# Sliding-window attention and a PReLU feed-forward on one core: the seven-product scheme begins one block earlier, and the sums it needs are made in borrowed rooms

## The chip, the cores and the metric
One core of a Trainium2 chip runs one program. The metric is device time in microseconds; the runs shown before the change gave 881.37, 882.29 and 882.43, median 882.29. The profiled execution took 882.02 us, of which 880.3 us lie between its first and last instruction (the span).

## The reference
```python
scores = scale * q @ k^T, masked to 0 <= i - j < 64      # 8 batches x 8 heads, 576 tokens, head 64
x = softmax(scores) @ v, heads side by side               # 4608 tokens x 512
h = x @ w_in                                              # 512 -> 2048
g = max(h, 0) + alpha * min(h, 0)
out = g @ w_out                                           # 2048 -> 512
```
Everything is fp32. The weights come as 64-bit numbers and are turned into fp32 in the kernel.

## The kernel before, in words
**Tiles and blocks.** The 4608 tokens are 36 tiles of 128; four tiles are a block, so there are 9 blocks, numbered 0 to 8 here ("the third block" is block 2). A block's hidden layer has 16 slices f of 128.

**Split numbers.** Each fp32 operand is held as a high part and a low part (`xh`/`xl`, `win_h`/`win_l`, `gh`/`gl`, ...), and a product is three matmuls: high-high, high-low, low-high.

**A cell** (`cell`, line 883) is one slice f of one block done plainly: 12 matmuls of 512 columns into one PSUM bank (line 896, called H here), then slopes on ACT (line 798), the PReLU on DVE (805), the high part on ACT (811), the low part on POOL (815), and 12 matmuls of 512 columns into the four output banks (line 832, called o).

**A pair** (`pair`, line 971) does two slices q = f/2 at once by a Strassen-like scheme: seven half products of 6 matmuls with 256 columns (line 1010, called P: 42 of them) in the place of eight. It uses two banks (`bx`, `by`), a few adds on DVE (1037), copies on ACT (1045, 1047), the sums of tokens that `attend` makes for a paired block (lines 726 to 776) and five entries of sums of `w_in`, 256 KB each, which are streamed from DRAM for each pair (line 988) into five rooms ("ring"). Four of these rooms are pieces of `win_h`/`win_l`, free once the sums 6 and 7 are made and the last plain block has used its slices 12 to 15; the fifth is a room of the eighth sum.

**The sums of `w_in`** (`combine(q)`, line 921, q = 0 to 7) each take four rooms of 128x512: two totals (930), four short DVE operations (935 to 938), two high parts on ACT (942), two low parts on POOL or DVE (945), and six stores to DRAM from SP's queue (950, 954).

**Blocks.** Block 0 and 1 get their attention in block 0 (t = 0 to 7) by PE transposes; weights are converted meanwhile. `W0 = 3`: blocks 0 to 2 are plain, blocks 3 to 8 paired.

**Visits.** From block 2 on the attention of a block is done inside earlier blocks, at two places of each (`stays`, lines 1130 to 1136, and 1160 to 1172). A visit is, in PE's order, the scores of one tile (64 small matmuls, line 578, called s), the values of two earlier tiles (64 matmuls, line 699, called AV), and the scores of another tile. `put_behind` fixes this order; a hidden slice two further on is put behind the visit's end.

**Who sets the order.** `Plan` is a list scheduler with a written cost of each step: it takes steps in order of time, hands out banks (four, `bank`: 4 to 7) and rooms, and the instructions are emitted in the order of its times. `take` and `give` are a step's rooms; `behind` fixes an order of starts, not of ends; `want` is a due time. The early steps have due times and first times written out (`DUE`, `BEGIN`, `HELD`). A tile's values hold their bank until its token operands are written (lines 710 to 776).

**The end.** Each block's four output tiles are copied (868, 870) and stored (873). The rooms ("os") are four at first; two are passed on to other uses by the eighth sum, so two are left for the last blocks.

Of the kernel before, what the change touches and what calls it, by code (L numbers as in the profile page):

```python
# [9 lines left out]
F32 = mybir.dt.float32  # L10
# [260 lines left out]

STAYS = (10, 2)
FAT = 10
W0 = 3
SHORT = 93.0
TSETS = (0, 3)
LAGS = (16.0, 19.0)
EARLY = (14.0, 18.0, 23.0, 28.0)
FIRST, PACE, TURN, LONG = 20.0, 5.6, 112.0, 97.0

# [2 lines left out]
def banded_attention_then_prelu_ffn(  # L283
# [65 lines left out]
    def weight(name, f):  # L349
        f0 = max(x for x in parts_of[name] if x <= f)  # L350
        return parts_of[name][f0][:, f - f0, :]

    xh = const.tile([P, NP, RING * P], F32R, name="xh")
    xl = const.tile([P, NP, RING * P], F32R, name="xl")

    stock = dict(bank=[4, 5, 6, 7], o=[0, 1, 2], q=["q0", "q1"], k=["k0", "k1"], v=["v0"], w=[0, 1],
                 mix=["pt0"], clean=[], pt=[], new=[], kk=[], T0=[], T1=[], ring=[], u2=[], u=[0, 1], reg0=[0], reg1=[1], ring6=[("h", 6)],
                 ring7=[("l", 6)], ring8=[("h", 7)], ring9=[("l", 7)], g=["g0", "g1"], gh=["gh0", "gh1", "gh2"], gl=["gl0", "gl1"],
                 raw=["u0", "u1", "u2"], val=["e0", "e1"], low=["e2", "e3"], os=[])
    pts = dict(pt0=const.tile([P, NH, P], F32, name="pt_0"))  # L360
# [4 lines left out]
    plan = Plan(stock)  # L365
    plan.stock["o"].append((WARM + 1.0, 3))
    spare = ps.tile([P, P], F32, tag="b3", name="spare")
    nought = xl[:, 0, (RING - 1) * P:].bitcast(F32)
    nc.vector.memset(nought, 0.0)
    plan.idle = lambda _: nc.tensor.matmul(spare, nought, nought, start=True, stop=True)  # L370
    step = plan.step
# [4 lines left out]
    def room(b, shape, dtype, name):  # L376
        return sb.tile(shape, dtype, tag=str(b.at), name=name)
# [103 lines left out]
    def attend(t, by_pe, want, loads_behind=(), behind=(), soon=math.inf):  # L481
# [218 lines left out]
                                         d["pt"][:, u * NP + e, h * W:(h + 1) * W], start=True, stop=True)  # L700

        def x_high(_):
            nc.scalar.copy(xh[:, :, xs], d["av"])

        def x_low(_):
            nc.vector.tensor_tensor(out=xl[:, :, xs], in0=d["av"], in1=xh[:, :, xs].bitcast(F32), op=ALU.subtract)  # L706
            if not paired:
                d.clear()

# [77 lines left out]
    def parts(t):  # L787

        return [slice(0, E // 2), slice(E // 2, E)] if t == NT - 1 else [slice(0, E)]

    def behind(ts, f, d, done, hb, want_o, cols, coarse=True):
# [68 lines left out]
        if f == NF - 1:  # L860
            for i, t in enumerate(ts):
                for x in parts(t):
                    sbuf, os = Buffer("os" if len(parts(t)) == 1 else "g", 1), {}

                    def copy(e, t=t, x=x, sbuf=sbuf, os=os):
                        os[0] = room(sbuf, [P, x.stop - x.start], F32, f"os_{t}_{x.start}")
                        if e == ACT:
                            nc.scalar.copy(os[0], po[t][:, x])
                        else:
                            nc.vector.tensor_copy(os[0], po[t][:, x])  # L870

                    def store(e, t=t, x=x, os=os):
                        (nc.scalar if e == ACT else nc.sync).dma_start(out[t * P:(t + 1) * P, x], os[0])

                    m = len(parts(t))
                    c = step({DVE: (0.33, 0.42)} if x.start else {ACT: (0.28, 0.39)} if m == 2 else
                             {ACT: (0.48, 0.59), DVE: (0.6, 0.69)}, copy, [whole[t]], take=[sbuf],
                             give=[ob[t]], want=want_o + 3 + i)
                    step({ACT: (0.4, 0.4)} if x.start else {SP: (0.4, 0.4)}, store, [c], give=[sbuf], moved=0.8 / m)
                    if t < NBLK:  # L880
                        begun.append(c)

    def cell(ts, f, want_h, want_o):
        plan.group = "c", f, ts[0]
        n = len(ts)
        nt = n * P
        d = {}
        xs = slice((ts[0] % RING) * P, (ts[0] % RING) * P + nt)
        hb = Buffer("bank", 1)

        def hidden(_):
            d["h"] = ph = bank(hb, [P, NBLK * P], F32, f"h_{ts[0]}_{f}")
            k = 0
            for wt, xt in (("win_h", xh), ("win_h", xl), ("win_l", xh)):
                for c in range(NP):
                    nc.tensor.matmul(ph[:, :nt], weight(wt, f)[:, c * P:(c + 1) * P], xt[:, c, xs],  # L896
                                     start=(k == 0), stop=(k == 3 * NP - 1))
                    k += 1

        xb = [st[t]["x"] for t in ts]  # L900
        s0 = step({PE: ({2: 1.46, 4: 2.72}[n], {2: 1.55, 4: 2.87}[n])}, hidden,
                  [st_done[t] for t in ts] + cv[2 * f]["done"], take=[hb], want=want_h)
        first[ts[0] // NBLK, f] = s0
        for b in xb:
            b.uses = NF
        s0.give += xb
        if ts[0] // NBLK == W0 - 1:
            s0.give += regions[f // 2]
        behind(ts, f, d, [s0], hb, want_o, range(n))
# [11 lines left out]
    def combine(q):  # L921
        plan.group = "s", q, 2 * NBLK
        d = {}
        bufs = [Buffer("os", 1, {2: "u2", 3: "ring"}.get(i) if q == NF // 2 - 1 else None) for i in range(4)]
        f = 2 * q
        done = [*cv[2 * f]["done"], *cv[2 * f + 2]["done"]]

        def total(e, i):
            d[i] = room(bufs[i], [P, E], F32, f"sum_{q}_{i}")
            (nc.gpsimd if e == POOL else nc.vector).tensor_tensor(  # L930
                out=d[i], in0=weight("win_h", f + i).bitcast(F32), in1=weight("win_l", f + i).bitcast(F32), op=ALU.add)

        def sums(_):
            a11, a12, a21, a22 = d[0][:, :2 * P], d[0][:, 2 * P:], d[1][:, :2 * P], d[1][:, 2 * P:]
            nc.vector.tensor_tensor(out=a22, in0=a21, in1=a22, op=ALU.add)
            nc.vector.tensor_tensor(out=a21, in0=a11, in1=a21, op=ALU.subtract)
            nc.vector.tensor_tensor(out=a11, in0=a22, in1=a11, op=ALU.subtract)
            nc.vector.tensor_tensor(out=a12, in0=a12, in1=a11, op=ALU.subtract)

        def high(i):  # L940
            d["h", i] = room(bufs[2 + i], [P, E], F32R, f"sum_h_{q}_{i}")
            nc.scalar.copy(d["h", i], d[i])

        def rest(e, i):
            (nc.gpsimd if e == POOL else nc.vector).tensor_tensor(
                out=d[i].bitcast(F32R), in0=d[i], in1=d["h", i].bitcast(F32), op=ALU.subtract)

        def keep(i, low):
            if i == 2:
                nc.sync.dma_start(entries[q][:, 0, low],  # L950
                                  region("win_l" if low else "win_h", q)[:, :2 * P].bitcast(F32))
            else:
                x = d[i] if low else d["h", i].bitcast(F32)
                nc.sync.dma_start(entries[q][:, 1 + 2 * i:3 + 2 * i, low], x.rearrange("p (e c) -> p e c", e=2))

        entries[q] = dram.tile([P, 5, 2, 2 * P], F32, name=f"kept_{q}")
        t0 = step({POOL: (1.22, 1.28), DVE: (0.59, 0.68)}, lambda e: total(e, 0), done, begun[-NBLK:],
                  take=bufs + taken.get(q, []), give=regions[q], port=True)
        begun.append(t0)
        t1 = step({POOL: (1.22, 1.28), DVE: (0.59, 0.68)}, lambda e: total(e, 1), [*done, t0], give=regions[q], port=True)  # L960
        su = step({DVE: (1.35, 1.45)}, sums, [t0, t1], port=True)
        out = [step({SP: (0.4, 0.4)}, lambda _, low=low: keep(2, low), done, [t0], give=regions[q], moved=0.6, span=0.8)
               for low in (0, 1)]
        for i in range(2):
            hi = step({ACT: (0.51, 0.61)}, lambda _, i=i: high(i), [su])
            lo = step({POOL: (1.22, 1.28), DVE: (0.59, 0.68)}, lambda e, i=i: rest(e, i), [hi], port=True)
            out.append(step({SP: (0.4, 0.4)}, lambda _, i=i: keep(i, 0), [hi], give=[bufs[2 + i]], moved=0.9))
            out.append(step({SP: (0.4, 0.4)}, lambda _, i=i: keep(i, 1), [lo], give=[bufs[i]], moved=0.9))
        kept[q] = out

    def pair(ts, q, want):
# [26 lines left out]
            return [weight("win_" + x, f + m)[:, k * 2 * P:(k + 1) * 2 * P] for x in "hl"]  # L998

        def tokens(k, where):  # L1000
            return [[x[:, 2 * k + c, where] for c in range(2)] for x in (xh, xl)]

        def turned(i):
            return [[region("win_" + x, q0 + i)[:, c * 2 * P:(c + 1) * 2 * P] for c in range(2)] for x in "hl"]
# [68 lines left out]

    tsets, loaded, last_p = {}, [], {}
    regions, taken, begun = {}, {}, []
    for i, q0 in enumerate(TSETS):
        b = Buffer(f"reg{i}", 3 * 6, f"T{i}")
        taken[q0] = [b]
        regions.update({q: [b] for q in range(q0, q0 + 3)})
# [55 lines left out]
    for n in range(NB):  # L1135
# [12 lines left out]
        for f in range(NF):  # L1148
# [11 lines left out]
            if (n, f) in stays:  # L1160
# [5 lines left out]
                    some.append(va)  # L1166

                end = last_p.get((n, f), first[n, f] if n == W0 - 1 else last_o[ts[0]])
                for x in [*row[:1], *prior, *row[1:]]:
                    put_behind(x, end)  # L1170
                    end = x
# [46 lines left out]
```

## Time and profile before

| | us |
|---|---|
| median of the runs | 882.29 |
| the profiled execution, and its span | 882.02, 880.3 |
| PE busy (share of the span) | 869.9 (99%) |
| DVE, ACT, POOL busy | 550.0, 453.0, 351.4 |
| chain that ended last: PE | 90% of the span |
| o matmuls on that chain (line 832) | 43% |
| P matmuls (line 1010), H matmuls (line 896) | 27%, 12% |

PE's busy time is the modelled one of pipelined matmuls; where it is 99%, what counts is how far apart the starts are. PE was granted its full clock through nearly the whole span.

### The profile page before, as it was taken

The numbers are of one execution on the slowest core, as the hardware profiler recorded it, in microseconds if no ns is written. First come the engines' busy times: TensorE is split into PE (matmuls) and PEld (weight loads), VectorE is DVE, ScalarE is ACT, GpSimd is POOL, SyncE is SP. The second block draws the span as 40 slices with busy tenths as digits, with TensorE's granted clock in tenths as the row PEclk, the third lists the DMA queues.
The fourth block names the chain that finished last, engine by engine and source line by source line (L and its number), as shares of the span: only waits on it lengthen the run. The fifth ranks groups of instructions, "written<-read, shape, count | busy, mean of one in ns | idle before, by whom it ended". The sixth has DMA issues, their size and how long they took to land.

```text
span 880.3 us, 20268 instructions
## 1 busy us (share of the span) xinstructions
PE 869.9 (99%) x7649; PEld 758.9 (86%) x7649; DVE 550.0 (62%) x1587; ACT 453.0 (51%) x1216; POOL 351.4 (40%) x315
## 2 busy tenths in 40 slices
PE   9999999999999999999999999999999999999997
PEld 8888788888878888989899989989898989999996
DVE  6989865979667737657583948394847575323221
ACT  7888765435443526363544545363636363434332
POOL 5878742856463323323241334233323332222221
PEclk9999999999999999999999999999999999999999
DMA  8656744255562247645764576547655664345441
GB/s 314 208 197 195 244 139 132 86 143 169 163 198 95 50 134 210 193 135 164 224 188 130 147 240 188 147 128 219 194 170 147 190 199 127 111 129 169 120 125 56
DMA packets 100978, 143.42 MB, mean 163 GB/s; under 512 B 8065, under 2 KB 63633, under 8 KB 100881
## 3 DMA queue, kind: packets, MB, share of 16 engines
q1 hardware_dynamic: 100144, 141.46, 52.8%
q8 instruction: 61, 1.00, 0.5%
q10 hardware_dynamic: 736, 0.66, 0.2%
q14 instruction: 37, 0.29, 0.1%
HBM read 122.17 MB, written 19.92 MB: 161 GB/s over the span
## 4 chain that ended last, share of the span: by engine, by line
PE 90%; DMA 3%; DVE 3%; ACT 2%; issue 1%; POOL 1%; SPq 0%; ACTq 0%; DVEq 0%; POOLq 0%
PE o L832 43%; PE h L1010 27%; PE h L896 12%; PE av L699 4%; PE s L578 3%; DMA raw<-w_in 1%; PE s L560 1%; DMA raw<-w_out 1%; PE spare L370 1%; PE t L656 1%; DMA out<-os 1%; DMA kept<-sum 1%; ACT w L608 0%; ACT two L403 0%; DVE two L413 0%
## 5 line engine op out<-in xcount | busy, mean ns | idle before, releaser
L815 POOL TENSOR_TENSOR gl<-g,gh 128x512 fp32r<-128x512 f32 x128 | 166.9, 1304 | 410.8 <-ACT gh L811 263.4
L832 PE MATMUL o<-wout_h,gh 128*128 128x512 f32 x576 | 227.8, 396 | 0.2 <-ACT gh L811 0.2
L832 PE MATMUL o<-wout_l,gh 128*128 128x512 f32 x576 | 225.5, 392 | 0.0
L798 ACT ACTIVATE g<-h,sa_sb 128x512 f32<-128x512 f32 (+1 forms) x148 | 100.2, 677 | 194.5 <-DVE h L1037 133.1
L832 PE MATMUL o<-wout_h,gl 128*128 128x512 f32 x576 | 160.3, 391 | 0.0
L805 DVE SCALAR_TENSOR_TENSOR g<-h,s_sb,g 128x512 f32<-128x512 f32 x128 | 95.8, 749 | 77.5 <-ACT g L798 76.7
L679 DVE STREAM_TRANSPOSE pt<-w 32x256 f32<-32x256 f32 x312 | 130.0, 428 | 7.0 <-POOL w L639 2.3
L832 PEld LDWEIGHTS o<-wout_h,gl 128*128 128x128 f32 x576 | 107.4, 188 | 23.5
L832 PEld LDWEIGHTS o<-wout_h,gh 128*128 128x128 f32 x576 | 108.4, 188 | 22.0 <-issue 0.5
L832 PEld LDWEIGHTS o<-wout_l,gh 128*128 128x128 f32 x576 | 108.4, 188 | 19.3
L811 ACT CAST gh<-g 128x512 fp32r<-128x512 f32 x128 | 79.3, 620 | 81.9 <-DVE g L805 81.8
L1037 DVE TENSOR_TENSOR h<-h,w 128x256 f32<-128x256 f32 x48 | 20.8, 433 | 128.7 <-PE h L1010 128.5
L639 POOL TENSOR_TENSOR w<-w,rc 128x768 f32<-128x768 f32 (+2 forms) x44 | 59.5, 1352 | 48.4 <-DVE rc L635 36.8
L618 ACT ACTIVATE w<-w,nm 128x96 f32<-128x96 f32 x208 | 76.2, 369 | 3.6 <-DVE nm L612 3.6
L1047 ACT COPY u<-h 128x256 f32<-128x256 f32 x96 | 35.8, 373 | 62.8 <-PE h L1010 62.1
L1010 PE MATMUL h<-win_h,win_l 128*128 128x256 f32 x288 | 59.7, 289 | 1.4 <-DMA win_l<-kept 1.4
L1037 DVE TENSOR_TENSOR h<-h,u 128x256 f32<-128x256 f32 x96 | 41.2, 429 | 30.3 <-PE h L1010 26.3
L1010 PE MATMUL h<-xh,win_h 128*128 128x256 f32 x288 | 57.7, 282 | 0.0
L896 PE MATMUL h<-xh,win_h 128*128 128x512 f32 (+1 forms) x208 | 53.6, 380 | 0.6 <-DVE xl L706 0.6
L896 PE MATMUL h<-xl,win_h 128*128 128x512 f32 (+1 forms) x208 | 52.3, 373 | 0.0
L896 PE MATMUL h<-xh,win_l 128*128 128x512 f32 (+1 forms) x208 | 52.2, 373 | 0.0
L1010 PEld LDWEIGHTS h<-xh,win_h 128*128 128x128 f32 x288 | 47.8, 191 | 3.6
(108 smaller groups left out, 1514.1 us busy)
## 6 DMA issues: line engine op xcount, KB each, us to landing
win_h<-kept SPq DMA_DIRECT2D x96, 256.0 KB, 2.8
win_l<-kept SPq DMA_DIRECT2D x95, 256.0 KB, 2.8
v<-vN SPq DMA_DIRECT2D x72, 256.0 KB, 4.7
k<-kT SPq DMA_DIRECT2D x35, 384.0 KB, 4.2
stream<-kept SPq DMA_DIRECT2D x49, 256.0 KB, 2.6
out<-os SPq DMA_DIRECT2D x35, 256.0 KB, 3.1
q<-qT SPq DMA_DIRECT2D x34, 256.0 KB, 4.2
raw<-w_in SPq DMA_DIRECT2D x16, 512.0 KB, 4.9
```

Source lines behind the costliest of these rows:

```text
L618: nc.scalar.activation(w, w, AF.Exp, scale=-1.0, bias=d["nm"][:, g:g + 1], accum_out=d["sm"][:, g:g + 1])
L639: nc.gpsimd.tensor_tensor(out=w, in0=w, in1=d["rc"][:, g].unsqueeze(2).broadcast_to(list(w.shape)), op=ALU.mult)
L679: nc.vector.transpose(dst[:, :, i * SUB:(i + 1) * SUB], d["w"][r, :, :, k * SUB:(k + 1) * SUB].rearrange("p e h k -> p (e h) k"))
L798: nc.scalar.activation(d["g"], d["h"][:, :nt], AF.Copy, scale=sa_sb[:, f:f + 1])
L805: nc.vector.scalar_tensor_tensor(out=g, in0=d["h"][:, :nt], scalar=s_sb[:, f:f + 1], in1=d["g"], op0=ALU.mult, op1=ALU.max)
L811: nc.scalar.copy(d["gh"], d["g"])
L815: (nc.vector if start else nc.gpsimd).tensor_tensor(out=d["gl"], in0=d["g"], in1=d["gh"].bitcast(F32), op=ALU.subtract)
L832: nc.tensor.matmul(po[t], gt[:, cols[i] * P:(cols[i] + 1) * P], weight(wt, f), start=(f == 0 and k == 0), stop=(f == NF - 1 and k == 2))
L896: nc.tensor.matmul(ph[:, :nt], weight(wt, f)[:, c * P:(c + 1) * P], xt[:, c, xs], start=(k == 0), stop=(k == 3 * NP - 1))
L1010: nc.tensor.matmul(out, a[:, c * P:(c + 1) * P], b[c], start=start and i == c == 0, stop=i == 2 and c == 1, skip_group_check=True)
L1037: nc.vector.tensor_tensor(out=out, in0=a, in1=b, op=ALU.add)
L1047: nc.scalar.copy(d["u"][i], d[x])
```

## The change
Block 2 is made of pairs instead of cells (`W0 = 2`). The sums 0 to 4 (`LENT = 5`) take their rooms from the token operands of block 0 (eight rooms, "xr", which can serve two sums at a time), start once block 0's last hidden slice and the last tokens of block 1 are begun, and hand block 2's token rooms x0 to x3 on only when all five are stored; the stores have due times (`DUES`). For that `xh` and `xl` are split in halves, one tile each for even and for odd blocks. The sums 5 to 7 keep their rooms. In blocks from `W0` on, the first step of a visit takes the banks of the visit's AV steps as well. The last but one output tile is copied to a room of `gh` instead of "os". By its formula `stays` also moves one visit of block 2 from slice 5 to slice 2, and the visits of block 1 are put behind a hidden slice instead of an output step.

```diff
-W0 = 3
+W0 = 2
+LENT = 5
+DUES = (165.0,165.0,165.0,180.0,180.0,180.0,190.0,190.0)
...
-    xh = const.tile([P, NP, RING * P], F32R, name="xh")
-    xl = const.tile([P, NP, RING * P], F32R, name="xl")
+    xs_of = {(x, half): sb.tile([P, NP, NBLK * P], F32R, tag=f"x{x}{half}", name=f"x{x}_{half}")
+             for half in (0, 1) for x in "hl"}
+    lent_of = {}
+    def tokens_of(x, where):
+        half, start = divmod(where.start, NBLK * P)
+        return xs_of[x, half][:, :, start:start + where.stop - where.start]
...
         def x_high(_):
-            nc.scalar.copy(xh[:, :, xs], d["av"])
+            if t == 2 * NBLK:
+                for x in "hl":
+                    xs_of[x, 0] = sb.tile([P, NP, NBLK * P], F32R, tag=f"x{x}0", name=f"x{x}_2")
+            nc.scalar.copy(tokens_of("h", xs), d["av"])
...
-                    sbuf, os = Buffer("os" if len(parts(t)) == 1 else "g", 1), {}
+                    sbuf, os = Buffer("g" if t == NT - 1 else "gh" if t == NT - 2 else "os", 1), {}
...
     def combine(q):
-        bufs = [Buffer("os", 1, {2: "u2", 3: "ring"}.get(i) if q == NF // 2 - 1 else None) for i in range(4)]
+        lent = q < LENT
+        bufs = [Buffer("xr" if lent else "os", 1, {2: "u2", 3: "ring"}.get(i) if q == NF // 2 - 1 else None)
+                for i in range(4)]
+        back = borrowed if lent else []
+        due = DUES[q]
+        def place(i, dtype):
+            if lent:
+                x, c = bufs[i].at
+                if not lent_of:
+                    for y in "hl":
+                        lent_of[y] = sb.tile([P, NP, NBLK * P], F32, tag=f"x{y}0", name=f"lent_{y}")
+                return lent_of[x][:, c].bitcast(dtype)
+            return room(bufs[i], [P, E], dtype, f"sum_{q}_{i}")
...
-        t0 = step({POOL: (1.22, 1.28), DVE: (0.59, 0.68)}, lambda e: total(e, 0), done, begun[-NBLK:],
-                  take=bufs + taken.get(q, []), give=regions[q], port=True)
-        begun.append(t0)
+        t0 = step({POOL: (1.22, 1.28), DVE: (0.59, 0.68)}, lambda e: total(e, 0), done,
+                  [first[0, NF - 1], st_done[2 * NBLK - 1]] if lent else begun[-NBLK:], take=bufs + taken.get(q, []) + (back if q == 0 else []),
+                  give=regions[q], port=True)
+        if not lent:
+            begun.append(t0)
...
-            out.append(step({SP: (0.4, 0.4)}, lambda _, i=i: keep(i, 0), [hi], give=[bufs[2 + i]], moved=0.9))
+            out.append(step({SP: (0.4, 0.4)}, lambda _, i=i: keep(i, 0), [hi], give=[bufs[2 + i]] + back, want=due, moved=0.9))
...
+    borrowed = [Buffer(f"x{i}", 4 * LENT) for i in range(NBLK)]
...
+                if n >= W0 and row:
+                    for va in prior:
+                        row[0].take += va.take
+                        va.take = []
```

## Rows read from the trace of the kernel before

**Rows 1.** The page: span, and busy time by engine.
```profile
span 880.3 us, 20268 instructions
PE 869.9 (99%) x7649; PEld 758.9 (86%) x7649; DVE 550.0 (62%) x1587; ACT 453.0 (51%) x1216; POOL 351.4 (40%) x315
```
**Rows 2.** Waits of PE: total us, times, longest us.
```profile
PE h L1010 <- DMA win_l<-kept: 1.4, 1, 1.4
...
PE h L896 <- DVE xl L706: 0.6, 1, 0.6
```
**Rows 3.** Chain that ended last, in time: start us, us, what; blocks 2 to 6.
```profile
226.40 2.72 PE h L896 x12
...
272.62 2.72 PE o L832 x12
...
323.19 2.15 PE h L1010 x18
...
390.46 3.86 PE o L832 x16
...
669.46 3.86 PE o L832 x16
...
740.89 4.37 PE h L1010 x36
...
751.46 4.37 PE h L1010 x36
```
**Rows 4.** Stretches: us, busy of PE, PEld, DVE, ACT, POOL, PEclk, DMA share, GB/s.
```profile
120.00:140.00 20.00, 20.00 (x120) 16.38 (x119) 7.66 (x11) 10.03 (x17) 7.66 (x7) 1.00 0.42 129
140.00:160.00 20.00, 20.00 (x145) 16.41 (x144) 15.49 (x62) 9.98 (x39) 8.32 (x10) 1.00 0.30 93
...
226.00:323.00 97.00, 96.44 (x770) 78.82 (x769) 61.87 (x171) 42.03 (x116) 41.23 (x37) 1.00 0.41 126
390.50:483.60 93.10, 93.10 (x913) 83.42 (x913) 59.46 (x179) 46.45 (x132) 30.13 (x28) 1.00 0.59 176
```
**Rows 5.** PE in time, a visit of paired blocks: start us, us, what, count.
```profile
385.39 1.00 PE L578 MATMUL s<-kk,q 64*32 64x96 f32 x64
386.32 0.50 PE L832 MATMUL o<-wout_h,gh 128*128 128x512 f32 x1
...
387.45 2.08 PE L699 MATMUL av<-pt,v 128*64 128x64 f32 x64
```
**Rows 6.** PE in time, two visits of block 1.
```profile
172.31 2.08 PE L699 MATMUL av<-pt,v 128*64 128x64 f32 x64
...
197.76 1.00 PE L578 MATMUL s<-kk,q 64*32 64x96 f32 x64
198.69 2.08 PE L699 MATMUL av<-pt,v 128*64 128x64 f32 x64
200.70 1.00 PE L578 MATMUL s<-kk,q 64*32 64x96 f32 x64
```
**Rows 7.** DVE in time, same visit as rows 5.
```profile
386.50 0.25 DVE L612 CUSTOM_DVE_ANT_0 w<-s,masks 128x96 f32<-128x96 f32 x1
...
387.92 0.74 DVE L805 SCALAR_TENSOR_TENSOR g<-h,s_sb,g 128x512 f32<-128x512 f32 x1
```
**Rows 8.** DVE in time, the last tokens of block 1.
```profile
128.91 0.69 DVE L706 TENSOR_TENSOR xl<-av,xh 128x512 fp32r<-128x512 f32 x1 [0.94 <-ACT xh L703]
```
**Rows 9.** The sums' instructions: duration ns min/median/max, first and last start.
```profile
L942 ACT CAST sum_h<-sum x16: 609/619/623, 153.7 to 273.4; 128x512 fp32r<-128x512 f32 x16
...
L936 DVE TENSOR_TENSOR sum<-sum,sum x8: 424/876/1575, 152.3 to 269.3; 128x256 f32<-128x256 f32 x8
```
**Rows 10.** All engines in time, the end of the program.
```profile
874.68 3.14 SPq L873 DMA_DIRECT2D out<-os  x3
...
876.41 0.37 ACTq L873 DMA_DIRECT2D out<-os  x1
876.88 0.58 ACT L868 COPY os<-o 128x512 f32<-128x512 f32 x1 [1.03 <-DVE os L870]
```

More of the change, by code (lines that the diff above doesn't have):

```diff
@@ L351, in weight @@
         return parts_of[name][f0][:, f - f0, :]
-    xh = const.tile([P, NP, RING * P], F32R, name="xh")
-    xl = const.tile([P, NP, RING * P], F32R, name="xl")
+    xs_of = {(x, half): sb.tile([P, NP, NBLK * P], F32R, tag=f"x{x}{half}", name=f"x{x}_{half}")
[4 more added lines that the diff above has]
+        return xs_of[x, half][:, :, start:start + where.stop - where.start]
     stock = dict(bank=[4, 5, 6, 7], o=[0, 1, 2], q=["q0", "q1"], k=["k0", "k1"], v=["v0"], w=[0, 1],
-                 mix=["pt0"], clean=[], pt=[], new=[], kk=[], T0=[], T1=[], ring=[], u2=[], u=[0, 1], reg0=[0], reg1=[1], ring6=[("h", 6)],
+                 mix=["pt0"], clean=[], pt=[], new=[], kk=[], T0=[], T1=[], ring=[], u2=[], u=[0, 1], xr=[(x, c) for x in "hl" for c in range(4)], reg0=[0], reg1=[1], ring6=[("h", 6)],
                  ring7=[("l", 6)], ring8=[("h", 7)], ring9=[("l", 7)], g=["g0", "g1"], gh=["gh0", "gh1", "gh2"], gl=["gl0", "gl1"],
@@ L367, in banded_attention_then_prelu_ffn @@
     spare = ps.tile([P, P], F32, tag="b3", name="spare")
-    nought = xl[:, 0, (RING - 1) * P:].bitcast(F32)
+    nought = xs_of["l", 1][:, 0, (NBLK - 1) * P:].bitcast(F32)
     nc.vector.memset(nought, 0.0)
@@ L702, in x_high @@
         def x_high(_):
-            nc.scalar.copy(xh[:, :, xs], d["av"])
+            if t == 2 * NBLK:
+                for x in "hl":
+                    xs_of[x, 0] = sb.tile([P, NP, NBLK * P], F32R, tag=f"x{x}0", name=f"x{x}_2")
+            nc.scalar.copy(tokens_of("h", xs), d["av"])
         def x_low(_):
-            nc.vector.tensor_tensor(out=xl[:, :, xs], in0=d["av"], in1=xh[:, :, xs].bitcast(F32), op=ALU.subtract)
+            nc.vector.tensor_tensor(out=tokens_of("l", xs), in0=d["av"], in1=tokens_of("h", xs).bitcast(F32),
+                                    op=ALU.subtract)
             if not paired:
@@ L893, in hidden @@
             k = 0
-            for wt, xt in (("win_h", xh), ("win_h", xl), ("win_l", xh)):
+            for wt, xt in (("win_h", "h"), ("win_h", "l"), ("win_l", "h")):
                 for c in range(NP):
-                    nc.tensor.matmul(ph[:, :nt], weight(wt, f)[:, c * P:(c + 1) * P], xt[:, c, xs],
+                    nc.tensor.matmul(ph[:, :nt], weight(wt, f)[:, c * P:(c + 1) * P], tokens_of(xt, xs)[:, c],
                                      start=(k == 0), stop=(k == 3 * NP - 1))
@@ L923, in combine @@
         d = {}
-        bufs = [Buffer("os", 1, {2: "u2", 3: "ring"}.get(i) if q == NF // 2 - 1 else None) for i in range(4)]
+        lent = q < LENT
+        bufs = [Buffer("xr" if lent else "os", 1, {2: "u2", 3: "ring"}.get(i) if q == NF // 2 - 1 else None)
+                for i in range(4)]
+        back = borrowed if lent else []
         f = 2 * q
+        due = DUES[q]
         done = [*cv[2 * f]["done"], *cv[2 * f + 2]["done"]]
+        def place(i, dtype):
[6 more added lines that the diff above has]
+            return room(bufs[i], [P, E], dtype, f"sum_{q}_{i}")
         def total(e, i):
-            d[i] = room(bufs[i], [P, E], F32, f"sum_{q}_{i}")
+            d[i] = place(i, F32)
             (nc.gpsimd if e == POOL else nc.vector).tensor_tensor(
@@ L940, in high @@
         def high(i):
-            d["h", i] = room(bufs[2 + i], [P, E], F32R, f"sum_h_{q}_{i}")
+            d["h", i] = place(2 + i, F32R)
             nc.scalar.copy(d["h", i], d[i])
@@ L966, in combine @@
             lo = step({POOL: (1.22, 1.28), DVE: (0.59, 0.68)}, lambda e, i=i: rest(e, i), [hi], port=True)
-            out.append(step({SP: (0.4, 0.4)}, lambda _, i=i: keep(i, 0), [hi], give=[bufs[2 + i]], moved=0.9))
-            out.append(step({SP: (0.4, 0.4)}, lambda _, i=i: keep(i, 1), [lo], give=[bufs[i]], moved=0.9))
+            out.append(step({SP: (0.4, 0.4)}, lambda _, i=i: keep(i, 0), [hi], give=[bufs[2 + i]] + back, want=due, moved=0.9))
+            out.append(step({SP: (0.4, 0.4)}, lambda _, i=i: keep(i, 1), [lo], give=[bufs[i]] + back, want=due, moved=0.9))
         kept[q] = out
@@ L1000, in tokens @@
         def tokens(k, where):
-            return [[x[:, 2 * k + c, where] for c in range(2)] for x in (xh, xl)]
+            return [[tokens_of(x, where)[:, 2 * k + c] for c in range(2)] for x in "hl"]
         def turned(i):
```

## The prediction
> **What bounds the kernel now.** I read the busy times first. PE is busy 869.9 us of a span of 880.3 and no other engine is over 62% [rows 1]. A busy share of 99% of pipelined matmuls says little by itself, so the waits of PE come next: after the start-up only two are worth naming, 1.4 us for a streamed sum and 0.6 us for a token operand that DVE wrote late [rows 2]. In the chain of waits, in order of time, PE's work then follows itself block after block. So the time is the sum of what PE issues, and a change is worth what it takes from that sum or puts between its parts.
>
> What the reader is to see in the chain: a plain and a paired block can be measured by their first matmuls. Block 2 begins at 226.40 (its first H) and block 3 at 323.19 (its first P), with one output step of the block before still to come at both: 96.79 us. Paired blocks repeat every (669.46 - 390.46) / 3 = 93.00 us [rows 3].
>
> **Block 2 by pairs: -3.8 us.** Two cells are four steps of 2.72 us, 10.88 us; a pair without a visit is 751.46 - 740.89 = 10.57 us [rows 3]. Eight of them save 8 x 0.31 = 2.5 us. The whole blocks differ by more, 96.79 - 93.00 = 3.79, since block 2 also has the 0.6 us wait of [rows 2] and a visit that is broken into three pieces. I take 3.8, the measured difference of blocks; the lower end is 2.5 (wait and broken visit come back elsewhere). The other engines carry it: per block DVE goes from 61.87 to 59.46 us, ACT from 42.03 to 46.45, POOL from 41.23 to 30.13, the DMA share from 0.41 to 0.59, all far from full; and PE's granted clock is 1.00 in both kinds of block [rows 4], so none of it comes from the clock.
>
> **The change-over from plain to paired: 0.** The 1.4 us wait [rows 2] belongs to it: the rooms of the streamed sums come free only as the last plain block ends, while its output stores go out. All of that moves one block forward unchanged. Ends: -1.6 (it vanishes) and +3 (twice as long again, with block 2's later loads beside it).
>
> **Visits that take all banks at once: -1.2 us.** Now a visit in a paired block is s, four o, AV, s: the values wait for banks that the pair just finished gives back, and o matmuls fill in. The four take 387.45 - 386.32 = 1.13 us [rows 5] where four of 2.72 / 12 make 0.91: 0.22 us for going from small to whole matmuls and back. With all banks in hand AV can follow s at once. Block 1 has such a visit, s, AV, s at 197.76, 198.69, 200.70 with nothing between [rows 6]. Eleven visits with scores lie in blocks 2 to 7, so at most 11 x 0.22 = 2.4 us go. Against it: the first scores wait until both banks of the pair are returned. In the trace the second return is at 387.92 + 0.74 = 388.66, behind 387.92 - 386.50 = 1.42 us of masks of these very scores [rows 7]; without those it is near 387.3, 1.9 us after 385.39. Behind the waiting step PE's queue holds the visit and the next pair; eight o of the pair before (1.8 us) can go ahead of it. Uncovered remains 0.1 us a visit; for the copies in between I allow up to 0.3, 3.3 us in all. Ends -2.4 and +3.3; I take half of the gain, nearer to the visit of [rows 6].
>
> **Sums made sooner: +1.0 us.** No sum is added; each is moved whole: two totals, four DVE operations, two ACT copies, two low parts, six stores. Before, the 16 copies run from 153.7 to 273.4 us, a sum per 17 us [rows 9]; now five should be stored by 165 to 180, all by 190. They can't begin before block 1's last tokens, 128.91 [rows 8]. The cover: from 120 to 140 us DVE and POOL are each idle 12.3 of 20 us, from 140 to 160 DVE 4.5 and POOL 11.7 [rows 4]. At 17 us apart two of the sums already lay ahead of the values at 172.31 [rows 6]; three more are 3 x 4 x 0.43 = 5.2 us of DVE, and 3 x 4 x 0.69 = 8.3 for totals and low parts if DVE does them all (0.69 is the like operation of [rows 8]). Against these 13.5 stand the 4.5 and the half of 12.3 that lies behind 129: 10.7 us, and POOL takes the rest. If the cover fails, this waits: DVE's queue holds the masks and transposes of tiles 8 and 9, their values hold two of four banks until x0 and x1 come back, and block 1's cells stand behind them. SP's queue gets the 30 stores earlier, ahead of loads that have time. Ends: 0; and 13.5 - 10.7 + 3.6 (three sums stretched by 1.2, below) - 2.7 (one cell step that can go ahead) = +3.7. I take 1.0: two sums in this stretch cost PE nothing.
>
> Here a rule of the Trainium skill speaks against the change. One of the four DVE operations takes 0.42 us at best, 0.88 in the median and 1.58 at worst [rows 9], so in about half of the sums it stood behind something of some 1.2 us. The page "SBUF — State Buffer", section "Who interferes with whom", says that a DVE instruction with two SBUF inputs and a POOL instruction that reads SBUF exclude each other for the whole length of the one that came first. Taken strictly, each of the four can meet that: 3 x 4 x 1.2 = 14 us instead of 3.6, and the sum would end at the third rival.
>
> **The end: -1.2 us.** Three stores leave SP's queue between 874.68 and 877.82, one leaves ACT's at 876.41; the last of SP's waits for a copy at 876.88, that of the last but one tile, which had no room until an earlier store had landed [rows 10]. With a room of `gh` its copy runs beside the others, and the last store is the one at 876.41 instead of about 877.5: 1.1 us, and it moves only half a tile. That half tile's own chain is late next, and stays. Ends -1.4 and -0.8.
>
> **Sum.** -3.8 + 0 - 1.2 + 1.0 - 1.2 = -5.2 us, from the profiled execution's 882.02 (span 880.3 and 1.7 around it) to 876.8. That execution lies 0.27 us below the median of the runs, so I forecast **877.0** for the median. Its own range, with the terms at moderate ends: 874.5 to 879.8.
>
> **Rivals.**
> *The visits eat the gain.* The pairs save 2.5 and the end 1.1, but the visits cost their 3.3: 882.3 - 2.5 - 1.1 + 3.3 + 1.0 = 883.0; with half of that cost, 881.3. For it: what is uncovered is a few tenths a visit, too small to be sure of. Against: o matmuls are at hand in [rows 5].
> *The sums come too late* (slower). All rooms of block 2's streams but one are pieces of `w_in` that the sums 6 and 7 must have read; the fifth is a room of sum 7. So a last sum later than about 226 us holds PE at the first pair, one us for each. At the old pace of 17 us from 129 on it comes at 265, and the time is 877 + 39 = 916. It bites from a pace of (226 - 129) / 8 = 12.1 us a sum and makes the kernel slower than before from 12.8; at 13 us, 233, it is 884. For it: DVE has 4.5 us of idle time in 20 from 140 on [rows 4]. Against: two sums fit in the borrowed rooms at once.
> *The pairs come, but block 1 loses as much*, by banks held for tiles 8 and 9 or by the strict rule above: 882.3 - 3.8 - 1.2 + 3.7 = 881.0, and 882 with the visits' gain turned to a small loss.
>
> **Chances.** A measurement of this kernel can tell about 0.2% (1.8 us) from no change, so faster is below 880.5 and slower above 884.1. Forecast 0.62 (0.60 faster, 0.02 same); visits eat the gain 0.18 (0.06 faster, 0.08 same, 0.04 slower); sums too late 0.08 (slower); block 1 loses as much 0.12 (0.04 faster, 0.07 same, 0.01 slower). Together 0.70, 0.17, 0.13. The range 874.0 to 882.0 takes in the forecast's own, the third rival and the lighter half of the first, and leaves out about 0.2.
>
> **What would show it.** In the chain: a first P near 226, block 2 about 93 us long, later blocks 92.5 to 93.0 with s, AV, s unbroken. In PE's waits: still one of 1 to 2 us for a streamed sum near 235, none near 264, none over 1 us from 130 to 215. The last copy of a sum before 200 instead of 273.4. The last store from ACT's queue. It is wrong if PE waits over 3 us before 230, or if a paired block takes more than 93.3 us.

## The result: slower, 887.0 us instead of 881.9

The changed kernel takes 887.03 us (median of 6 runs, 884.27 to 888.33), the kernel before 881.90 beside it (6 runs): ratio 1.0056, 95% interval 1.0039 to 1.0073. Forecast were 877.0 and "faster". The profiled execution took 886.64 us, with a span of 884.9. One execution among the experiments below, the profiled one of zero_fill14, is left out of that run's median: all its matmuls, from the start, lay 0.84 us apart, and it took 2998.62 us.

The page and the waits of PE (total us, times, longest us) of the kernel after:
```profile
span 884.9 us, 20749 instructions
PE 871.1 (98%) x7793; PEld 766.5 (87%) x7793; DVE 570.9 (65%) x1628; ACT 464.3 (52%) x1245; POOL 346.3 (39%) x311
```
```profile
PE h L907 <- DVE nm L619: 3.3, 1, 3.3
PE h L1036 <- ACT u L1073: 1.7, 1, 1.7
...
PE av L706 <- DVE nm L619: 0.9, 1, 0.9
```
Beside [rows 2] the first and the third are new: PE waits for banks that DVE's masks (L619) give back, once for 3.3 us. The second stands where the 1.4 us for a streamed sum stood (11.8 us behind the first P, 11.5 before), but its releaser is a copy on ACT (L1073).

PE in time, after: the last values of block 0, the scores of the visit at 167, three of the nine groups of four H behind the long wait, the first P, and a visit of paired blocks:
```profile
127.44 1.15 PE L706 MATMUL av<-pt,v 128*64 128x64 f32 x32
...
167.34 0.32 PE L585 MATMUL s<-kk,q 64*32 64x96 f32 x2 [0.56 <-issue]
167.95 0.98 PE L585 MATMUL s<-kk,q 64*32 64x96 f32 x62 [0.29 <-DVE g L816]
...
184.86 2.05 PE L907 MATMUL h<-xh,win_h 128*128 128x512 f32 x4 [3.34 <-DVE nm L619]
186.70 1.91 PE L907 MATMUL h<-xl,win_h 128*128 128x512 f32 x4
...
193.22 1.07 PE L907 MATMUL h<-xh,win_h 128*128 128x512 f32 x4
...
235.40 0.40 PE L1036 MATMUL h<-xh,win_h 128*128 128x256 f32 x2
...
300.34 1.00 PE L585 MATMUL s<-kk,q 64*32 64x96 f32 x64
301.27 2.09 PE L706 MATMUL av<-pt,v 128*64 128x64 f32 x64
303.28 1.00 PE L585 MATMUL s<-kk,q 64*32 64x96 f32 x64
```
I call "block 1" the time from the last values of block 0 to the first product of block 2: 235.40 - 127.44 = 107.96 us. In the trace of before it is 226.24 - 127.10 = 99.14 (226.24 is the first matmul of the piece that [rows 3] starts at 226.40). **Block 1 lost 8.8 us**, with the same 864 matmuls in the same forms in both stretches: all of it is waiting and pace. From the first product of block 2 to the last matmul it is 645.5 us instead of 648.8, and from there to the end of the span 4.05 instead of 5.3. The sum, 8.8 - 3.3 - 1.3 = +4.2, and a start 0.34 later make the 4.6 us between the spans. So of the 6.2 us of gains that were forecast (3.8, 1.2 and 1.2) 4.6 came; one stretch of 25 us, 166 to 191, took more than all of them.

What stands in that stretch: DVE in time, after, from the end of sum 5 on, and POOL in time beside it:
```profile
174.79 0.42 DVE L962 TENSOR_TENSOR sum<-sum 128x256 f32<-128x256 f32 x1
175.13 1.26 DVE L641 TENSOR_SCALAR rc<-sm 128x8 f32<-128x8 f32 x1
...
176.55 0.70 DVE L816 SCALAR_TENSOR_TENSOR g<-h,s_sb,g 128x512 f32<-128x512 f32 x1
177.16 1.36 DVE L959 TENSOR_TENSOR lent_h<-lent_h 128x256 f32<-128x256 f32 x1
178.56 1.40 DVE L960 TENSOR_TENSOR lent_h<-lent_l,lent_h 128x256 f32<-128x256 f32 x1
179.99 1.40 DVE L961 TENSOR_TENSOR lent_l<-lent_h,lent_l 128x256 f32<-128x256 f32 x1
181.43 1.37 DVE L962 TENSOR_TENSOR lent_l<-lent_l 128x256 f32<-128x256 f32 x1
...
183.93 0.25 DVE L619 CUSTOM_DVE_ANT_0 w<-s,masks 128x96 f32<-128x96 f32 x1
```
```profile
176.78 1.47 POOL L646 TENSOR_TENSOR w<-w,rc 128x768 f32<-128x768 f32 x1 [0.41 <-DVE rc L642]
178.21 1.47 POOL L826 TENSOR_TENSOR gl<-g,gh 128x512 fp32r<-128x512 f32 x1
179.64 2.88 POOL L969 TENSOR_TENSOR sum<-sum,sum 128x512 fp32r<-128x512 f32 x2
```
The four operations of sum 4 take 1.36 to 1.40 us where sum 5's, just before, take 0.42. Each ends about 0.3 us after a POOL operation has ended (178.25, 179.68, 181.10, 182.52), and the next POOL operation begins before it ends: the two engines take turns. Behind the sum stand two low parts and then the masks of tile 11, at 183.93, which give PE its bank.

Two stretches (us, busy of PE, PEld, DVE, ACT, POOL, PEclk, DMA share, GB/s) of after, block 1's and two half blocks of pairs:
```profile
180.00:200.00 20.00, 16.66 (x61) 13.23 (x60) 17.81 (x49) 7.98 (x25) 9.98 (x10) 0.83 0.57 184
...
439.80:532.80 93.00, 92.99 (x913) 83.58 (x912) 59.71 (x179) 46.46 (x132) 30.07 (x29) 1.00 0.60 176
```
The granted clock fell to 0.83 on the mean from 180 to 200: after the idle 3.34 us the first 14 H come 0.427 us apart, the lower of PE's two levels (1.2 GHz), the rest 0.227 (2.4 GHz). That is 14 x 0.20 = 2.8 us on top.

The end, after:
```profile
879.23 2.48 ACT L879 COPY os<-o 128x512 f32<-128x512 f32 x4 [5.29 <-PE o L843]
879.84 2.22 SPq L884 DMA_DIRECT2D out<-os  x4
881.81 0.42 DVE L881 COPY os<-o 128x256 f32<-128x256 f32 x1 [8.58 <-ACT os L879]
882.26 0.37 ACTq L884 DMA_DIRECT2D out<-os  x1
```
The last store is ACT's now; no copy waits for a room as in [rows 10].

### The profile page after: what moved, and what is told of

Read it like the earlier page. It is cut to its first block, busy times and chain, and to the rows that moved or that the text cites. A ratio compares the mean times of both kernels' runs of the same rounds, so it can differ in the third digit from the quotient of the medians.

```text
span 884.9 us, 20749 instructions
## 1 busy us (share of the span) xinstructions
PE 871.1 (98%) x7793; PEld 766.5 (87%) x7793; DVE 570.9 (65%) x1628; ACT 464.3 (52%) x1245; POOL 346.3 (39%) x311
## 4 chain that ended last, share of the span: by engine, by line
PE 92%; DVE 5%; DMA 1%; ACT 1%; issue 1%; POOL 0%; SPq 0%; ACTq 0%; DVEq 0%; POOLq 0%
PE o L843 42%; PE h L1036 31%; PE h L907 9%; PE av L706 4%; PE s L585 3%; PE s L567 1%; DVE pt L689 1%; PE spare L377 1%; PE t L663 1%; DMA k<-kT 1%; DMA out<-os 0%; DVE lent_h L960 0%; DVE lent_h L959 0%; DVE g L816 0%; DVE w L609 0%
## 5 line engine op out<-in xcount | busy, mean ns | idle before, releaser
L1063 DVE TENSOR_TENSOR h<-h,w 128x256 f32<-128x256 f32 x56 | 24.2, 433 | 142.4 <-PE h L1036 141.8
L1036 PE MATMUL h<-xh,win_l 128*128 128x256 f32 x556 | 95.9, 283 | 0.0
L1073 ACT COPY u<-h 128x256 f32<-128x256 f32 x112 | 41.8, 373 | 76.2 <-PE h L1036 76.2
L1036 PEld LDWEIGHTS h<-xh,win_l 128*128 128x128 f32 x556 | 80.4, 192 | 0.9
L1063 DVE TENSOR_TENSOR h<-h,u 128x256 f32<-128x256 f32 x112 | 48.0, 429 | 30.2 <-PE h L1036 24.8
L1036 PE MATMUL h<-xh,win_h 128*128 128x256 f32 x340 | 66.0, 281 | 0.0
L1036 PEld LDWEIGHTS h<-xh,win_h 128*128 128x128 f32 x340 | 58.3, 189 | 8.0
L1036 PE MATMUL h<-win_h,win_h 128*128 128x256 f32 x252 | 51.3, 285 | 0.0
L1036 PE MATMUL h<-win_h,stream 128*128 128x256 f32 x224 | 47.8, 295 | 1.8 <-ACT u L1073 1.7
```

What stands on the lines that cost most here:

```text
L1036: nc.tensor.matmul(out, a[:, c * P:(c + 1) * P], b[c], start=start and i == c == 0, stop=i == 2 and c == 1, skip_group_check=True)
L1063: nc.vector.tensor_tensor(out=out, in0=a, in1=b, op=ALU.add)
L1073: nc.scalar.copy(d["u"][i], d[x])
```

## The experiments

Twelve runs of eleven kernels (zero_fill14 and zero_fill14b are one). "Block 1" and "rest" (first product of block 2 to the last matmul) are read from each profiled execution as above; the ratio is to runs of the kernel before beside each, whose median was 881.90 to 882.29.

| kernel | median us | ratio (95%) | block 1 | rest |
|---|---|---|---|---|
| before | 881.90 | 1 | 99.1 | 648.8 |
| after | 887.03 | 1.0056 (1.0039 to 1.0073) | 108.0 | 645.5 |
| tail_only | 880.97 | 0.9977 (0.9963 to 0.9991) | 99.1 | 649.3 |
| visits_only | 882.72 | 0.9994 (0.9980 to 1.0007) | 99.2 | 648.7 |
| order_sum4 | 884.30 | 1.0018 (1.0008 to 1.0028) | 104.1 | 645.4 |
| zero_fill | 888.17 | 1.0057 (1.0044 to 1.0070) | 107.7 | 647.3 |
| zero_fill14 | 888.49 | 1.0077 (1.0057 to 1.0096) | | |
| zero_fill14b | 886.39 | 1.0042 (1.0023 to 1.0062) | 106.0 | 645.7 |
| no_visits | 886.65 | 1.0046 (1.0030 to 1.0062) | 105.2 | 646.6 |
| sums_pool_34 | 880.90 | 0.9987 (0.9976 to 0.9998) | 101.8 | 644.6 |
| order_all | 883.64 | 1.0016 (1.0006 to 1.0026) | 106.0 | 645.9 |
| order_all2 | 883.12 | 1.0010 (0.9997 to 1.0022) | 104.5 | 645.8 |
| banks_free | 890.42 | 1.0092 (1.0073 to 1.0111) | 109.7 | 647.0 |
| values_behind | 879.43 | 0.9967 (0.9954 to 0.9981) | 101.2 | 644.9 |

**Parts of the change alone.** The rooms of the last outputs, and the visits' taking of all banks, each put into the kernel before:
```diff
-                    sbuf, os = Buffer("os" if len(parts(t)) == 1 else "g", 1), {}
+                    sbuf, os = Buffer("g" if t == NT - 1 else "gh" if t == NT - 2 else "os", 1), {}
```


> The kernel before with one part of the change alone: the last but one output tile is copied to a room of gh. By the prediction 1.2 us are gone (1.1 of the last store's time, a bit more for its half size): ratio 0.9986, the stretch from the last matmul to the end 3.7 us instead of 4.9. Rival (the end is hidden or something else is late there): no change, ratio 1.0000.

> The kernel before with one part of the change alone: a visit in blocks 3 to 7 takes all its banks at its first step. By the prediction s, AV, s follow each other without o matmuls between, 0.22 us less for each of 9 visits, 0 to 2 us in all: ratio 0.998 to 1.000, period of two visits 46.3 instead of 46.5 us. Rival (the wait for the banks shows): PE waits some tenths before or in each visit, period 46.5 to 46.8, ratio 1.000 to 1.003.

The end alone gave -2.0 us (0.9977 x 881.9; interval -3.3 to -0.8), and in its profile 4.05 us from the last matmul to the end, as in after, instead of 5.3. The visits alone gave nothing that can be told from zero. In their profile the visits are unbroken, s, AV, s, but lie as far apart as before: from 343.4 to 715.5 us in eight half blocks, 46.5 each. Six of the eight are 46.30 to 46.37 us long, as forecast; the other two, 47.17 and 46.83, take the gain back. In the first of the two PE waits 0.50 us within the second scores. Taken out of the changed kernel (its block 1 is below):

> The changed kernel without the visits' wait for all their banks. Theory (that wait gains nothing: alone it measured 0.9994): 886.5 to 887.5 us, distance of the visits from 300 to 719 unchanged at 46.5 us. Rival (in blocks worked by pairs throughout the wait costs, since it keeps banks from the products): 0.2 us less per visit, 884.5 us.

886.65 us against 887.03: again not to be told from zero.

**Sum 4 behind tile 11's masks.** The order is a sorted list of planned starts; five steps of sum 4 get later ones (702 is the four DVE operations):
```diff
+LATER = {702: 179.30, 705: 181.96, 709: 181.97, 707: 183.00, 711: 183.10}
+        for i, t in LATER.items():
+            self.steps[i].start = t
```


> The changed kernel with one thing in another order: the four DVE operations of sum 4 (and its copies and two stores behind them) come after tile 11's masks in DVE's queue instead of before. No work is added or left out. Theory (the lock): in the changed kernel those four operations took 5.6 us instead of 1.7, each held by a POOL operation; the masks behind them came at 183.9 instead of about 178, PE waited 3.3 us for the bank, and the clock's fall behind that idle time cost another 2.8. Then PE's wait near 181 and the half-speed matmuls behind it are gone: 6 us less than the changed kernel, about 881, ratio to the kernel before 0.998 to 1.000. Rival (too much work): DVE and POOL simply have more to do from 160 to 200 than they can, and the delay comes out at the next visit or at tile 8's token operands: no gain, ratio 1.004 to 1.007.

884.30 us, block 1 3.9 us shorter, no slow matmuls. The wait moved; DVE in time and PE's waits:
```profile
177.76 1.63 DVE L974 TENSOR_TENSOR lent_l<-lent_l 128x512 fp32r<-128x512 f32 x1
179.31 1.78 DVE L974 TENSOR_TENSOR lent_h<-lent_h,lent_l 128x512 fp32r<-128x512 f32 x1
181.02 0.25 DVE L624 CUSTOM_DVE_ANT_0 w<-s,masks 128x96 f32<-128x96 f32 x1
```
```profile
PE h L912 <- DVE g L821: 2.3, 1, 2.3
```
The stretch passed to whatever of two SBUF inputs stood next: the low parts of sum 3 took 1.63 and 1.78 us instead of 0.68, beside POOL. The masks came at 181.0, and PE's wait became one for a PReLU at 187, behind seven transposes. So I moved those low parts and the PReLU too:

> As the run with sum 4 and the low parts of sum 3 behind tile 11's masks and the PReLU of chunk 7 ahead of seven transposes, with the two stores of sum 3's low halves put behind the low parts that they store. Theory (that run's waits at 192.4 and 196.9, 0.6 and 1.75 us, are the banks held by tiles 8 and 9, which come back no sooner whatever VectorE's order): the wait at 187 stays away, 1.5 us or more in all at 190 to 198, 883 to 884.5 us. Rival (they came from the two stores): no wait over 0.5 us at 190 to 198, 881 to 882 us.

883.12 us; the wait at 187 is gone, and 0.62 and 1.75 us of idle, which end at 192.6 and 198.3, stand in its place. A first form of this kernel, order_all, has two stores of sum 3 ahead of the low parts that they store, so it keeps something else than those low parts and computes another result; only its times can be used. It gave 883.64, with the same two waits; its block 1 is 1.5 us longer because the 64 matmuls of AV at 169.6 took 3.62 us instead of 2.08 (granted clock 0.53 from 169.6 to 173.2). Its expectation:

> The changed kernel with sum 4's four operations and the low parts of sum 3 on VectorE behind tile 11's masks, and the PReLU of chunk 7 of block 1 ahead of seven transposes of tile 10 instead of behind them. Theory (the wait that stayed at 187.3, 2.27 us, when sum 4 alone was put behind was the PReLU standing behind the transposes): no wait over 1 us between 175 and 192, first product of block 2 about 2 us sooner than the 232.3 there, 882 to 883 us. Rival (banks held): the same wait comes back behind the next group of matmuls, within 5 us, and the first product of block 2 stays within 0.5 us of 232.3; 884 us.

Of that text both sides held in part. There is no wait over 1 us between 175 and 192, as the theory said; but the first product of block 2 comes at 232.4 in order_all2 and 233.2 in order_all, not 2 us sooner than 232.3, and a wait came back soon behind the old one, as the rival said. These orders moved the wait on. That banks held are behind these later waits, as the theory of order_all2 has it, was not tested.

**Sums 3 and 4 on GpSimd**, which takes them off the contended engine:
```diff
-        su = step({DVE: (1.35, 1.45)}, sums, [t0, t1], port=True)
+        su = step({POOL: (2.7, 2.76)} if 3<=q<=4 else {DVE: (1.35, 1.45)}, sums, [t0, t1], port=True)
```


> The changed kernel with the four operations that make sums 3 and 4 on GpSimd instead of VectorE, which then has nothing of sum 4 between the masks of tile 10 and those of tile 11 but its reciprocal. Theory (VectorE's operations were stretched from 0.42 to 1.4 us each by GpSimd's beside them, tile 11's masks came at 183.9 instead of about 178, and the matmul engine stood 3.3 us and was slow behind it): no wait over 1.5 us between 175 and 195, no matmuls at 0.43 us behind it, first product of block 2 at about 228 to 230, 879 to 881 us. Rival (the two banks held by the values of tiles 8 and 9 are the cause, and they come back later still when GpSimd makes the sums): a wait of 2 us or more stays at 180 to 195, 885 us or more.

880.90 us. POOL in time, sum 4, and PE's waits:
```profile
176.00 0.74 POOL L960 TENSOR_TENSOR lent_h<-lent_h 128x256 f32<-128x256 f32 x1
176.82 0.74 POOL L961 TENSOR_TENSOR lent_h<-lent_l,lent_h 128x256 f32<-128x256 f32 x1
177.64 0.74 POOL L962 TENSOR_TENSOR lent_l<-lent_h,lent_l 128x256 f32<-128x256 f32 x1
178.46 0.74 POOL L963 TENSOR_TENSOR lent_l<-lent_l 128x256 f32<-128x256 f32 x1
```
```profile
PE av L706 <- DVE nm L619: 0.9, 1, 0.9
PE h L1037 <- DMA win_h<-kept: 0.9, 1, 0.9
PE s L585 <- issue: 0.6, 1, 0.6
```
DVE in time, the first of tile 11's masks:
```profile
180.61 0.26 DVE L619 CUSTOM_DVE_ANT_0 w<-s,masks 128x96 f32<-128x96 f32 x1 [3.69 <-PE s L585]
```
The slower engine makes the sum in 3.2 us where DVE needed 5.6. DVE stood idle for 3.69 us before tile 11's masks, PE's wait of 3.3 us and the slow matmuls are gone, and block 1 is 6.2 us shorter: the theory's case, though the two banks are held through all of this stretch (tile 8's values are made from 171.9 on and fetched from their bank only at 195.0; in after, 169.9 and 199.0). That the stretching and not the mere work made DVE late is worked out from the rows of after, and no run has sum 4 on DVE without POOL beside it: without the 3.8 us too long in sum 4 and the 1.1 in the row at 175.13 its masks would have come at about 179.0 instead of 183.9, where PE has made their scores by 178.5. What is left of block 1's loss, 2.6 us, is about the three short waits of the visit at 167, which this run has as well (0.57, 0.29 and 0.92).

**Are the held banks a cause of their own?** The values of tiles 8 and 9 put behind two more groups of H, sum 4 left on DVE:
```diff
+LATER = {799: 185.40, 837: 185.41, 838: 185.42}
+LATER.update({874: 185.43, 875: 185.44, 914: 185.45, 915: 185.46})
+LATER.update({896 + i: 185.47 + i * 1e-3 for i in range(12)})
```


> The changed kernel with the values of tiles 8 and 9 (with the loads behind them and the transposes of tile 10) moved behind two more groups of products of block 1, so that the two banks that they hold are free from 169 to about 185; sum 4 stays on VectorE. Theory (VectorE's late masks stop the matmul engine only because two of four banks are held by those values): the four operations of sum 4 still take about 1.4 us each and tile 11's masks still come at about 184, but the wait of 3.3 us at 181 is gone or below 1 us and no matmul takes 0.43 us; first product of block 2 at 229 to 231, 881 to 883 us. Rival (late VectorE alone is the cause, the banks don't matter): a wait of over 2 us comes back within 5 us of the old place, 886 us or more.

890.42 us, slower than after. DVE in time, PE in time, and PE's waits:
```profile
176.80 1.36 DVE L966 TENSOR_TENSOR lent_h<-lent_h 128x256 f32<-128x256 f32 x1
...
183.55 0.24 DVE L626 CUSTOM_DVE_ANT_0 w<-s,masks 128x96 f32<-128x96 f32 x1
```
```profile
176.93 1.25 PE L592 MATMUL s<-kk,q 64*32 64x96 f32 x62 [2.27 <-DVE g L823]
...
179.13 0.63 PE L850 MATMUL o<-wout_h,gh 128*128 128x512 f32 x1
```
```profile
PE s L592 <- DVE g L823: 2.6, 2, 2.3
PE h L914 <- DVE g L823: 2.3, 1, 2.3
PE h L914 <- DVE nm L626: 2.1, 1, 2.1
```
My theory was that late masks hurt only because two banks are held. It fell: with those banks free the masks are as late, and PE still waits 2.1 us for them, beside two new waits for PReLUs on the same DVE. Part of the 890.42 is the clock: behind the waits that end at 176.9 and at 249.0 (2.27 and 1.86 us) stand matmuls at half speed (granted clock 0.66 from 176.93 to 182.00, 0.58 from 248.97 to 253.00), where I had expected none. Together with sums_pool_34, where the banks stay held and PE does not wait: the late DVE is the cause; the held banks alone are not.

**The slow matmuls.** 24, then 14 matmuls by zeros, which add nothing to any bank, ahead of the waiting H:
```diff
+        for i in range(ZEROS):
+            s = Step({PE: (0.11, 0.11)}, self.zero, (), (), (), (), math.inf, 0.0, 0.0, False)
+            s.start, s.end, s.engine = ZERO_AT + i * 1e-4, ZERO_AT, PE
+            self.steps.append(s)
```


> The changed kernel with 24 small matmuls of zero weights (they add nothing to the outputs) put on PE just before the H that waits 3.3 us near 181, so that PE works through most of that wait. Theory (the clock falls because PE stood idle): the H matmuls behind it run at 0.227 us each instead of 0.427, 2.8 us less, ratio to the kernel before 1.002 to 1.004, while the wait itself stays. Rival (the clock falls for another reason, the idle time has no part in it): the 14 slow matmuls stay, ratio 1.005 to 1.007.

> The changed kernel with 14 matmuls by zeros ahead of the waiting group of block 1; 24 took 5.2 us, 1.9 more than the wait, so 14 take 3.0 and end before the bank comes free. They add nothing to any bank. Theory (the 14 slow matmuls behind the wait, 2.8 us, are the engine's clock that fell over an idle of 3.3 us): no matmuls at 0.43 us behind it, first product of block 2 at about 232.6 instead of 235.4, 884 us. Rival (the slow ones are a cost of the operands, x rooms or weights, in use at that time): 14 matmuls at 0.43 us stay, 887 us.

> The run with 14 matmuls by zeros once more, for a trace: its times were 885.97 to 890.78 us, where 884 had been expected. Theory (the clock falls over an idle; the zeros end before the bank comes): no slow matmuls, first product of block 2 at 232.6. Rival (the zeros cost more than their time, by what they hold of the engine's queue or of the bank): first product at 235 or later, though the matmuls run at 0.227 us.

With 24 the zeros ran 5.2 us, longer than the wait; the H behind them were fast, and nothing was won. Of the first run of 14 (888.49 us) there is no trace that can be read. In the second (886.39 us) the zeros end at 185.3 and the H are fast; block 1 is 2.0 us shorter than in after where I expected 2.8, and the first product of block 2, at 233.8, lies between theory (232.6) and rival (235). The medians of the two runs, 888.49 and 886.39 against 887.03, don't show the gain. PE in time behind the zeros, and in no_visits, where PE idles with no zeros at all:
```profile
185.56 1.17 PE L917 MATMUL h<-xh,win_h 128*128 128x512 f32 x4 [0.28 <-DVE nm L629]
```
```profile
184.00 1.17 PE L907 MATMUL h<-xh,win_h 128*128 128x512 f32 x4 [3.39 <-DVE nm L619]
```
```profile
180.00:200.00 20.00, 16.61 (x73) 13.43 (x72) 19.42 (x54) 9.60 (x27) 11.06 (x12) 1.00 0.58 184
```
The last fence is the stretch of no_visits that answers to the one of after: an idle of 3.39 us, and the granted clock stays at 1.00. So the slow matmuls are not the operands' doing, and they come behind such an idle in one execution and not in another; what decides is open. It is not the length alone: behind 2.27 us the clock fell in banks_free and stayed in order_sum4. The mean granted clock of each execution is on record: all six of after have 0.995 to 0.998, all ten of zero_fill and zero_fill14b 0.999 or more, the eleven of no_visits 0.995 to 1.000; of these the four at 0.997 or less took 887.30 to 889.06 us, the other seven 881.65 to 887.51. The two traces' blocks 1, 107.96 and 105.25, differ by 2.7 us, about these 2.8.

**A version that beats both.** Sums 3 and 4 on GpSimd, and the values of tiles 8 and 9 (799, 837, and the loads that need their rooms) behind one group of o, which needs no bank:
```diff
+LATER = {799: 173.45, 837: 173.46, 874: 173.47, 875: 173.48, 914: 173.49, 915: 173.50}
```


> Sums 3 and 4 made on GpSimd (as in the run that came to 880.9), and the values of tiles 8 and 9 behind one group of output products, where the matmul engine needs no bank. Theory (the three waits at 168 to 172, 0.57, 0.29 and 0.92 us idle, are for banks, and the last of them falls when other work stands ahead of the values): the 0.92 goes, the others stay; 1 us less than 880.9, 879 to 880.5 us. Rival (what comes behind, the masks and transposes of tile 10, then waits as long): 880.9 us within 0.5.

879.43 us, -2.9 against before (interval -4.1 to -1.7). PE's waits behind the start-up and the first P:
```profile
PE h L1042 <- DMA win_h<-kept: 0.9, 2, 0.7
...
PE s L590 <- DVE g L821: 0.3, 1, 0.3
```
```profile
228.34 0.40 PE L1042 MATMUL h<-xh,win_h 128*128 128x256 f32 x2
```
The 0.9 us for AV is gone. Block 1 costs 2.1 us more than before, the rest 3.8 less, the end 1.3 less: -3.0, near what was measured. From sums_pool_34 it can't be told for sure (the intervals of the ratios overlap), nor from tail_only: of the change, the end alone brings most of what is left.

## Why the prediction was wrong

**The failed step: "Sums made sooner: +1.0 us", with an end of +3.7.** Block 1 lost 8.8 us, and with sums 3 and 4 off DVE 6.2 of them went. I worked out how much work DVE and POOL have room for, from 129 to 160, and let a late DVE cost PE only the excess. In the kernel after only three of the sums were made by 160; the four operations of sums 3 and 4 ran from 171.7 to 182.8, in a stretch whose room I had not counted. There it was a chain: an addition ahead of a reciprocal that took 1.26 us instead of 0.17, four stretched operations, 4 x 0.96 = 3.8 us too long, and behind them the masks that give PE its bank. Of the 8.8, 8.7 are the wait of 3.34 with its refilling (3.6), the slow matmuls (2.8) and three short waits in the visit at 167 (2.3). These three are not the doing of sums 3 and 4, since they stay in sums_pool_34. That visit is one of those that the change puts behind a hidden slice instead of an output step, which the prediction gave no price; no run takes that part out, so whether it makes them is not shown. I had priced the third rival by the same arithmetic, so it came out at 881 to 882 too; its place was right, its size was not. Nor did I have the clock as a term at all: I wrote that none of it comes from the clock, from rows of stretches in which PE does not stand idle.

**The rule that I weighed.** In the kernel after, the 23 sum operations on DVE with no POOL operation beside them took at most 0.43 us; of the 9 with one, 7 took 1.36 to 2.13. The page "SBUF — State Buffer" of the Trainium skill, section "Who interferes with whom", which says that a DVE operation with two SBUF inputs and a POOL operation reading SBUF exclude each other, agrees with these rows and with the 0.3 us behind each POOL operation. Before, 6 of the 32 took 1.32 to 1.58 us: the number hardly rose. What differed is how many came in a row (two at most before, four in sum 4) and what stood behind them: before, the two longest, 1.58, came at 204 us (that of [rows 9]) and at 271, and PE waited for nothing of DVE's behind either. A count of stretched operations, mine or the strict one, could not have told the loss.

**Block 2 by pairs, -3.8, and the change-over, 0: as forecast, within what can be read.** The rest is 3.3 us shorter; with the change-over's 1.69 us of idle against 1.4 that is a block about 3.6 us shorter. The rest differs between traces, though: in the changed kernel and its variants it is 644.6 to 647.3, so one pair of traces tells the gain only to a microsecond or two. The change-over's wait was forecast for a streamed sum; in after it was released by a copy on ACT. Visits lie 93.1 us apart (300.3 to 393.4), against 93.0 before.

**The visits, -1.2: about 0.** They are unbroken as I said. Where nothing waits, a half block is about 0.1 us shorter, half of the 0.22 that I had worked out, and a few half blocks with a wait pay that back; two runs, alone and taken out, show no change. The upper end, +3.3, and with it the first rival, did not come either.

**The end, -1.2: right**, -1.3 in the traces, -2.0 (-3.3 to -0.8) in the times.

**The second rival** (sums too late for block 2's first pair) did not decide: the last copy of a sum began at 229.4, later than the 200 that I expected, and PE waited 1.7 us at the change-over.

The sign I had named for being wrong, "PE waits over 3 us before 230", is what happened.

## What to carry to other kernels

Work moved into another engine's idle time is not free by the sum of busy times: look for the instructions behind it in that engine's queue which release the bound engine, and price the moved work at its stretched duration in front of them. Where two engines exclude each other, giving a short operation to the slower one can be faster than letting it wait its turn on the quicker one. And an idle of a few us on the matmul engine can cost nearly as much again in clock behind it, in some executions and not in others.

## What the runs showed of the hardware

DVE's operations on the PReLU, with one input in PSUM, were never stretched: in the kernel after, the 71 of 128x512 beside POOL took 0.75 us in the median and 0.76 at most. But a TENSOR_SCALAR of 128x8, with a single SBUF input, took 1.26 us beside POOL (the row at 175.13) instead of 0.17; the eleven others beside POOL took 0.29 to 0.68. POOL's own four operations of a sum take 0.74 us each, less than twice DVE's undisturbed 0.42. And two idles of 3.34 and 3.39 us at the same place gave a granted clock of 0.83 and of 1.00 over the 20 us around them; an idle of 1.86 us (banks_free, 249.0) was followed by matmuls at half speed, one of 2.27 (order_sum4, 190.0) by none.
